# Each attention score matmul in two 32x64 tiles instead of one 32x128 tile

## The chip, the cores and the metric

One core of a Trainium2 chip runs the kernel. The metric is the time of one execution on the device, in microseconds (us). A profile was taken of one execution with the hardware profiler. TensorE (PE) does the matmuls and loads their weights (PEld), VectorE (DVE), ScalarE (ACT) and GpSimd (POOL) work on tiles in the on-chip memories, and SyncE (SP) issues DMAs.

## The reference

Two transformer layers, each windowed attention and then a feed-forward part, with the same weights in both layers. Sequence 2048, model width 576, 32 heads of 18, a window of 256 keys, feed-forward width 4608. The inputs are bf16.

```python
def _A_ref(x, wqkv, wo):
    B, S, D = x.shape
    H = 32; Dh = D // H; W = 256
    qkv = (lambda x, *d: x.transpose(*d))((x @ wqkv).reshape(B, S, 3, H, Dh), 2, 0, 3, 1, 4)
    q, k, v = qkv[0], qkv[1], qkv[2]
    scores = jnp.einsum("bhqd,bhkd->bhqk", q, k) * (Dh ** -0.5)
    idx = jnp.arange(S)
    mask = (idx[:, None] - idx[None, :] >= 0) & (idx[:, None] - idx[None, :] < W)
    scores = jnp.where(mask[None, None], scores, -1e9)
    p = _softmax(scores, axis=-1)
    o = jnp.einsum("bhqk,bhkd->bhqd", p, v)
    return (lambda x, *d: x.transpose(*d))(o, 0, 2, 1, 3).reshape(B, S, D) @ wo
...
    x = x + _A_ref(_layernorm(x, axis=-1), A_wqkv, A_wo)
    x = x + _B_ref(_layernorm(x, axis=-1), B_w1, B_b1, B_w2, B_b2)
```

`_B_ref` is a second layernorm, a matmul to 4608, gelu, and a matmul back to 576. The last two lines come twice.

## The kernel before

**Tiling.** The sequence is cut into chunks of 512 queries (four tiles of 128), four per layer, eight in all. For a chunk the kernel does layernorm and transposes, queries, keys and values (`qkv`, matmuls at lines 779, 782, 798 and 838), attention (`E`, made of `scores` and `pv`), the output projection and residual (`tail`), the first feed-forward matmul with gelu in three parts (`G_part`, matmuls at line 1074), and the second in three parts (`mm2`, through the helper `quad`, lines 779 and 782). Parts of neighbouring chunks are interleaved, so that attention of one chunk stands among feed-forward work of the one before.

**Scores.** Heads are laid out 32 partitions apart: group `g` of eight holds four heads, head `j` in partitions 32j to 32j+31 of `qT` and `kT` (18 of them are values, the others are zero). A task of `scores` takes one group and one unit of blocks. A unit is one or two parts, each one key tile of 128 keys against one, two or three neighbouring query tiles: 384 and 128 columns, 256 and 256, or, at a layer's start, 384 alone or 256 and 128. For each part four matmuls (line 907) run side by side in four row tiles of TensorE: head `j` in rows 32j, all 128 keys as its columns, written to a PSUM bank of its own (`bs[j // 2]` is a pair of banks). Such four are called a set below. The weights are the keys, the moving operand is the queries. ScalarE then takes the exponential of each pair of banks (line 916) into `pT`, GpSimd masks diagonal blocks and blocks at the window's edge (line 937), and `pv` (line 954) multiplies with the values in four column tiles: head `j` writes partitions 32j to 32j+19, 20 columns of weights, of which one is ones and gives the sum of the softmax.

**Other tile shapes.** Line 779 uses the whole array (128 x 128) and line 782 the same work in four column tiles of 128 x 32; `quad` takes one or the other by what stands next to it. Lines 838 and 1074 use two row tiles of 64 x 128, which share the contraction of 576 in halves. The page writes a shape as rows*columns of the weights ahead of the moving operand's.

**Order.** Work is added as tasks to a planner (`Plan`). Each has an estimated cost, data dependences, a priority with a written-out nudge by stage, and a mode that stands for its tile shape ("r" for scores, "c" for column tiles, "h" for two row tiles, "f" for the whole array); a change of mode adds 0.095 us to the estimate. The planner sorts the tasks into one fixed order per engine and gives each PSUM banks; the estimates decide nothing at run time. A task's matmuls are issued together, and the last of them signals the task's semaphore. Its waits stand before the first.

Of the kernel before, what the change touches and what calls it, by code (L numbers as in the profile page):

```python
# [40 lines left out]
class Sched:  # L41
# [23 lines left out]
    def add(self, eng, fn, reads=(), writes=(), dma=None, ring=4, own=False):  # L65
        waits = {}

        def want(ev):
            c, v, _e = ev
            if waits.get(c, 0) < v:  # L70
                waits[c] = v

        for r in reads:
            lw = self.last_write.get(r)
            if lw is not None and not (eng == "pe" and lw[2] == "pe"):
                want(lw)
        for w in writes:
            for rd in self.readers.get(w, ()):
                if own or rd[2] != eng or rd[3]:
                    want(rd[:3])  # L80
            lw = self.last_write.get(w)
            if lw is not None and (own or not (eng == "pe" and lw[2] == "pe")):
                want(lw)
        if dma is None:
            assert eng != "sp"
            c = self.cnt[eng]
            amount = 1
        else:
            rg = self.ring(eng, dma, ring)
            c = rg.sems[rg.i % rg.k]  # L90
            rg.i += 1
            amount = 16
            if c.val > 0:
                want((c, c.val, None))
        wl = []
        wd = self.waited[eng]
        for cc, v in waits.items():
            if wd.get(cc, 0) >= v:
                continue
            wd[cc] = v  # L100
            wl.append((cc, v))
        c.val += amount
        by = None if dma is not None else eng
        ev = (c, c.val, by)
        self.steps[eng].append(Step(eng, fn, wl, c, amount))
        for w in writes:
            self.last_write[w] = ev
            self.readers[w] = []
        for r in reads:
            self.readers.setdefault(r, []).append((c, c.val, by, dma is not None))  # L110
        return ev
# [323 lines left out]
def build_kernel(nc, A_x, A_wqkv, A_wo, B_x, B_w1, B_b1, B_w2, B_b2, out):  # L435
# [158 lines left out]
    def two(b):  # L594
        return ps[:, b.no * 512:(b.no + 2) * 512].rearrange("p (j c) -> p j c", j=2)
# [18 lines left out]
    def q_of(k):  # L614
        return (qx, "qx") if k == 1 else (qT, "q")

    def k_of(A):

        if Q1 <= A < Q1 + 2:
            return kx[:, A - Q1, :, :], f"kx{A - Q1}"  # L620
        sl = A if A < Q1 else (A - 2) % KS
        return kT[:, :, sl, :], f"k{sl}"
# [273 lines left out]
    def scores(k, g, parts, prio):  # L896
        l, t0, nt = CH[k]
        T0 = l * NT + t0
        qs, qname = q_of(k)
        sl = slots.popleft()  # L900
        bs = [Bank(SC, True), Bank(SC, True)]

        def fn(e):
            ins = None
            for (so, qo, nq, col) in parts:
                for j in range(4):
                    ins = e.matmul(two(bs[j // 2])[:, j % 2, col:col + nq * 128], k_of(T0 + so)[0][32 * j:32 * j + 32, g, :],  # L907
                                   qs[32 * j:32 * j + 32, g, qo * 128:(qo + nq) * 128], start=True, stop=True, tile_position=(32 * j, 0))
            return ins
        rd = [f"{qname}{qo + i}" for (so, qo, nq, col) in parts for i in range(nq)] + [k_of(T0 + p[0])[1] for p in parts]  # L910
        ncol = sum(p[2] for p in parts) * 128
        add("pe", fn, reads=rd, writes=bs, cost=0.01 + ncol * 0.00042, prio=prio, lat=0.15, alloc=bs, fifo="pa", mode="r", after=[f"p{sl}h{h}" for h in range(2)] + [f"p{sl}m{m}" for m in range(3)])
        lo = min(p[3] for p in parts)
        hi = max(p[3] + p[2] * 128 for p in parts)
        for h2 in range(2):
            add("act", lambda e, h2=h2: e.activation(pT[:, sl, 2 * h2:2 * h2 + 2, lo:hi], two(bs[h2])[:, :, lo:hi],  # L916
                                                     ACT.Exp, scale=SCALE),
                reads=[bs[h2]], writes=[f"p{sl}h{h2}"], cost=0.07 + 2 * (hi - lo) * 0.00083, lat=0.17,
                fifo="act", prio=prio)
        blk = {}  # L920
        for (so, qo, nq, col) in parts:
            for q in range(nq):
                if qo + q == so:
                    blk[col + q * 128] = "d"
                elif qo + q == so + 2:
                    blk[col + q * 128] = "o"
        runs = []
        for c in sorted(blk):
            if runs and runs[-1][0] == blk[c] and runs[-1][1] + runs[-1][2] * 128 == c:
                runs[-1][2] += 1  # L930
            else:
                runs.append([blk[c], c, 1])
        for mi, (kind, col, nb) in enumerate(runs):
            sgn = 1 if kind == "d" else -1
            pat = [[0, 4]] + ([[0, nb]] if nb > 1 else []) + [[sgn, 128]]
            ap = pT[:, sl, :, col:col + nb * 128]
            add("pool", lambda e, ap=ap, pat=pat, sgn=sgn, kind=kind: e.affine_select(  # L937
                ap, ap, pattern=pat, compare_op=(ALU.is_ge if kind == "d" else ALU.is_gt), fill=0.0, base=0, channel_multiplier=-sgn),
                reads=[f"p{sl}h0", f"p{sl}h1"], writes=[f"p{sl}m{mi}"], cost=0.12 + 0.475 * nb, prio=prio)
        return sl  # L940
# [373 lines left out]
```

## Time and profile before

| | |
|---|---|
| median of three runs | 863.52 us (863.37 to 866.63) |
| the profiled execution's own time | 865.5 us |
| its span, from the first to the last instruction | 863.7 us |
| granted TensorE clock | 1.000 |
| TensorE matmuls, busy | 849.0 us, 12056 |
| ScalarE, busy | 593.3 us |
| VectorE, busy | 391.1 us |
| GpSimd, busy | 378.7 us |
| line 907 (scores), matmuls | 1216, and 192 more whose operands lie in other tiles |

A row of a group names line, engine, operation, the tiles written and read, the shape, the number of instructions, then busy time and the mean ns of one, then idle time of the engine just before them with what ended it. Busy time counts overlapping instructions once. Matmuls are pipelined and the end of each is modelled, so rows of the timeline overlap by some 0.1 to 0.2 us; starts are what to compare. A row of a single line in a short window gives the minimum, median and maximum duration in ns. The row of waits gives total us, number and longest.

### The profile page before, as it was taken

The page shows a single profiled execution, that of the slowest core. Times are in us where ns is not written, and L with a number is a line of the kernel's source. Part 1 is how long each engine was busy: PE and PEld are TensorE (multiplying, and loading weights), DVE is VectorE, ACT ScalarE, POOL GpSimd, SP SyncE. Part 2 cuts the span into 40 slices and gives each one's busy share as a digit, 9 for nine tenths or more (in the row PEclk, how much of TensorE's full clock was granted, in tenths as well). Part 3 has the DMA queues.
Part 4 walks back from the last instruction along what each step waited for, and adds up shares of the span by engine and source line. Part 5 has one row for each costly group of instructions (what it writes and reads, how often), then busy time and mean ns, then how long its engine had stood idle before and what let it go on. Part 6 is the DMA issues. An engine that isn't in the chain of part 4 may idle for free.

```text
span 863.7 us, 27936 instructions
## 1 busy us (share of the span) xinstructions
PE 849.0 (98%) x12056; PEld 523.2 (61%) x12056; DVE 391.1 (45%) x934; ACT 593.3 (69%) x741; POOL 378.7 (44%) x560
## 2 busy tenths in 40 slices
PE   9899999999999999999999999999999999999998
PEld 7555556656556565565655665756556655656556
DVE  5879324645227542393424832655234434244012
ACT  5986787868767588573875776737787589872730
POOL 3876544565135653264421863425454276222100
PEclk9999999999999999999999999999999999999999
DMA  9598445351585715947359443684536953455320
GB/s 238 139 201 145 122 126 148 107 162 45 164 175 112 165 43 165 189 108 170 92 149 215 107 122 124 112 180 99 172 97 127 297 141 108 134 162 147 123 83 28
DMA packets 181866, 119.83 MB, mean 139 GB/s; under 512 B 107440, under 2 KB 181744, under 8 KB 181744
## 3 DMA queue, kind: packets, MB, share of 16 engines
q1 hardware_dynamic: 181744, 118.05, 54.8%
q8 instruction: 95, 1.56, 0.8%
q14 instruction: 27, 0.22, 0.1%
HBM read 90.10 MB, written 2.36 MB: 107 GB/s over the span
## 4 chain that ended last, share of the span: by engine, by line
PE 92%; DMA 2%; POOL 2%; ACT 2%; issue 1%; DVE 1%; POOLq 0%; ACTq 0%
PE ps L1074 32%; PE ps L779 28%; PE ps L782 11%; PE ps L838 9%; PE ps L907 6%; PE ps L954 5%; DMA xnTa<-xn 2%; POOL pT L937 2%; ACT pT L916 1%; PE ps L798 1%; PE ps L681 1%; DMA qT<-qn 1%; DVE oq L965 0%; ACT hT L1084 0%; PE ps L672 0%
## 5 line engine op out<-in xcount | busy, mean ns | idle before, releaser
L937 POOL TENSOR_SCALAR_AFFINE_SELECT pT<-pT 128x512 bf16<-128x512 bf16 (+1 forms) x368 | 284.0, 793 | 255.8 <-ACT pT L916 250.7
L916 ACT ACTIVATE pT<-ps 128x1024 bf16<-128x1024 f32 (+1 forms) x384 | 345.1, 973 | 59.1 <-PE ps L907 58.5
L1074 PE MATMUL ps<-xnTm,w_sb 64*128 64x512 bf16 x2592 | 290.5, 376 | 1.1 <-DVE x_res L1017 0.3
L1084 ACT ACTIVATE hT<-ps,b1col 128x512 bf16<-128x512 f32 x276 | 167.6, 688 | 174.9 <-PE ps L1074 174.4
L1074 PEld LDWEIGHTS ps<-xnTm,w_sb 64*128 64x128 bf16 x2592 | 128.3, 94 | 143.4 <-issue 6.9
L779 PE MATMUL ps<-w_sb,hT 128*128 128x288 bf16 x1410 | 188.8, 287 | 0.0
L1017 DVE TENSOR_TENSOR x_res<-ps,x_res 128x288 f32<-128x288 f32 x224 | 100.1, 450 | 189.0 <-PE ps L779 160.2
L779 PEld LDWEIGHTS ps<-w_sb,hT 128*128 128x128 bf16 x1410 | 130.8, 98 | 48.6 <-issue 15.1
L782 PE MATMUL ps<-w_sb,hT 128*32 128x288 bf16 x2808 | 96.2, 286 | 1.5 <-issue 1.4
L838 PE MATMUL ps<-wqkv,xnTa 64*128 64x288 bf16 x1296 | 91.3, 283 | 2.0 <-DMA xnTa<-xn 1.8
L965 DVE STREAM_TRANSPOSE oq<-ps 128x512 f32<-128x512 f32 x64 | 45.7, 715 | 99.5 <-PE ps L954 98.9
L859 DVE CAST qn<-ps 128x288 bf16<-128x288 f32 x120 | 49.0, 451 | 81.5 <-PE ps L838 66.5
L782 PEld LDWEIGHTS ps<-w_sb,hT 128*32 128x32 bf16 x2808 | 72.4, 97 | 16.6 <-issue 5.8
L838 PEld LDWEIGHTS ps<-wqkv,xnTa 64*128 64x128 bf16 x1296 | 61.8, 94 | 31.0 <-DMA xnTa<-xn 2.7
L907 PE MATMUL ps<-qT,kT 32*128 32x384 bf16 (+2 forms) x1216 | 64.1, 276 | 1.5 <-ACT pT L916 0.9
L694 DVE BATCH_NORM_STATS2 st_all<-x_res 128x6 f32<-128x288 f32 (+1 forms) x128 | 53.5, 442 | 5.0 <-DMA x_res<-in_A_x_dram 4.1
L1090 POOL TENSOR_TENSOR x_res<-x_res,b2bc 128x576 f32<-128x576 f32 x32 | 40.2, 1277 | 32.8 <-ACT hT L1084 32.8
L846 DVE CAST vA<-ps 128x288 bf16<-128x288 f32 x64 | 26.7, 451 | 61.7 <-PE ps L838 59.9
L707 POOL TENSOR_SCALAR vtmp<-mv_all 128x1 f32<-128x1 f32 (+1 forms) x43 | 8.9, 208 | 102.2 <-DVE mv_all L698 99.4
L954 PE MATMUL ps<-pT,vA 128*20 128x384 bf16 (+2 forms) x1408 | 50.4, 275 | 1.0 <-POOL pT L937 0.7
L907 PEld LDWEIGHTS ps<-qT,kT 32*128 32x128 bf16 x1216 | 19.4, 92 | 41.8 <-issue 26.6
L954 PEld LDWEIGHTS ps<-pT,vA 128*20 128x20 bf16 x1408 | 28.0, 91 | 18.5 <-issue 6.4
(58 smaller groups left out, 481.6 us busy)
## 6 DMA issues: line engine op xcount, KB each, us to landing
w_sb<-in_B_w_dram SPq DMA_DIRECT2D x46, 864.0 KB, 6.2
w_sb<-in_B_w_dram SPq DMA_DIRECT2D x48, 768.0 KB, 4.8
w_sb<-in_B_w_dram SPq DMA_DIRECT2D x96, 48.0 KB, 4.5
wqkv<-in_A_wqkv_dram SPq DMA_DIRECT2D x3, 576.0 KB, 4.5
x_res<-in_A_x_dram SPq DMA_DIRECT2D x3, 576.0 KB, 4.8
wqkv<-in_B_w_dram SPq DMA_DIRECT2D x2, 864.0 KB, 5.5
out_dram<-x_res SPq DMA_DIRECT2D x12, 144.0 KB, 2.0
wo_sb<-in_A_wo_dram SPq DMA_DIRECT2D x4, 144.0 KB, 3.2
```

The lines of the kernel that those rows point to most:

```text
L694: add("dve", lambda e, i=i, s=s: e.bn_stats(st_all[:, t, i, :], s[:, t, i * HB:(i + 1) * HB]), reads=res, writes=[f"st{t}_{i}"], cost=0.37 ...
L779: return e.matmul(bank(b)[:, 0:HB], lhs, rhs, start=start, stop=stop, skip_group_check=True)
L782: ins = e.matmul(bank(b)[32 * j:32 * j + 32, 0:HB], lhs[:, 32 * j:32 * j + 32], rhs, start=start, stop=stop, tile_position=(0, 32 * j), sk ...
L838: ins = e.matmul(bank(bs[o])[:, 0:HB], xnTa[r:r + 64, c, i * 128:(i + 1) * 128], wqkv[r:r + 64, c, col:col + HB], start=(c == 4), stop=(ph ...
L859: add("dve", lambda e, b=bs[o], dst=dst: e.tensor_copy(dst, heads_of(bank(b))), reads=[bs[o]], writes=[f"qn{sl}h{o}"], cost=0.375, lat=0.1 ...
L907: ins = e.matmul(two(bs[j // 2])[:, j % 2, col:col + nq * 128], k_of(T0 + so)[0][32 * j:32 * j + 32, g, :], qs[32 * j:32 * j + 32, g, qo * ...
L916: add("act", lambda e, h2=h2: e.activation(pT[:, sl, 2 * h2:2 * h2 + 2, lo:hi], two(bs[h2])[:, :, lo:hi], ACT.Exp, scale=SCALE), reads=[bs ...
L937: add("pool", lambda e, ap=ap, pat=pat, sgn=sgn, kind=kind: e.affine_select(ap, ap, pattern=pat, compare_op=(ALU.is_ge if kind == "d" else ...
L954: ins = e.matmul(bank(bo)[32 * j:32 * j + VW, qo * 128:(qo + nq) * 128], vA[:, (T0 + so) % VS, 8 * j + g, :], pT[:, sl, j, col:col + nq * ...
L1017: add("dve", lambda e: e.tensor_tensor(x_res[:, t, sl], bank(b)[:, 0:HB], x_old[:, t, sl], ALU.add), reads=[b] + ([f"xin{t}"] if first els ...
L1074: ins = e.matmul(bank(bks[i])[:, 0:n], w1_sb[r:r + 64, sls[i], col:col + 128], xnTm[r:r + 64, k % 2, c, 0:n], start=(c == 4), stop=(ph == ...
L1084: add("act", lambda e, ff=ff, hd=hd, bk=bk: e.activation(hd[:, 0:n], bank(bk)[:, 0:n], ACT.Gelu_apprx_tanh, bias=b1col[:, ff:ff + 1]), rea ...
```

## The change

In `scores`, each matmul becomes two. The first computes the lower 64 keys and writes partitions 0 to 63, the second the upper 64 keys and partitions 64 to 127, of the same bank and the same columns. Their tile position is row 32j and column 0 or 64. The moving operand (the queries) is the same for both. The task's cost, waits, banks and place in the order are as before, and so is all that reads the scores. A set has eight matmuls and eight weight loads instead of four and four.

```diff
                 for j in range(4):
-                    ins = e.matmul(two(bs[j // 2])[:, j % 2, col:col + nq * 128], k_of(T0 + so)[0][32 * j:32 * j + 32, g, :],
-                                   qs[32 * j:32 * j + 32, g, qo * 128:(qo + nq) * 128], start=True, stop=True, tile_position=(32 * j, 0))
+                    for u in range(2):
+                        ins = e.matmul(two(bs[j // 2])[64 * u:64 * u + 64, j % 2, col:col + nq * 128],
+                                       k_of(T0 + so)[0][32 * j:32 * j + 32, g, 64 * u:64 * u + 64],
+                                       qs[32 * j:32 * j + 32, g, qo * 128:(qo + nq) * 128], start=True, stop=True, tile_position=(32 * j, 64 * u),
+                                       skip_group_check=True)
```

## The prediction

> **What bounds the kernel now.** I read the page's engine rows first, then its groups, then the timeline of TensorE alone, then single lines inside short windows, then what TensorE waits for.
>
> ```profile
> PE 849.0 (98%) x12056; PEld 523.2 (61%) x12056; DVE 391.1 (45%) x934; ACT 593.3 (69%) x741; POOL 378.7 (44%) x560
> PEclk9999999999999999999999999999999999999999
> q8 instruction: 95, 1.56, 0.8%
> L907 PE MATMUL ps<-qT,kT 32*128 32x384 bf16 (+2 forms) x1216 | 64.1, 276 | 1.5 <-ACT pT L916 0.9
> ```
>
> TensorE is busy 98% of the span at full granted clock, and no other engine passes 69%. A busy share can hide pipelining, so I checked that the stream is really dense. The timeline shows it:
>
> ```profile
> 310.81 0.29 PE L838 MATMUL ps<-wqkv,xnTa 64*128 64x288 bf16 x2
> 311.03 0.40 PE L907 MATMUL ps<-qT,kT 32*128 32x256 bf16 x8
> 311.35 0.83 PE L954 MATMUL ps<-pT,vA 128*20 128x384 bf16 x24
> 312.01 1.65 PE L782 MATMUL ps<-w_sb,hT 128*32 128x288 bf16 x48
> 313.59 0.40 PE L907 MATMUL ps<-qT,kT 32*128 32x384 bf16 x8
> 313.92 1.65 PE L779 MATMUL ps<-w_sb,hT 128*128 128x288 bf16 x12
> 315.50 0.40 PE L907 MATMUL ps<-qT,kT 32*128 32x384 bf16 x8
> ```
>
> Starts are the numbers to use, since modelled ends overlap the next burst. From 312.01 to 313.59, 48 matmuls in four column tiles (12 sets) take 1.58 us; from 313.92 to 315.50, 12 full-width ones take 1.58 us too. Instruction by instruction the trace gives 122.5 ns from set to set in both: 288 columns at 2.4 per ns plus 2.5 ns. So four column tiles stream truly side by side. A score task (8 matmuls in 2 sets of four row tiles, 512 columns) holds TensorE from 311.03 to 311.35, 0.32 us: 213 ns of streaming, and the rest is the change of tile shape. Adding columns and the changes of shape accounts for almost the whole span, so any nanosecond added to a score task goes to the end.
>
> Count of tasks: 1216 + 128 + 64 = 1408 score matmuls (the rows by shape) make 352 sets in 192 tasks; each task has another tile shape before it and after it.
>
> **The change, part by part.** Nothing is moved: task order, waits, buffers and the instruction order of every engine stay, since the planner's costs are untouched. 1408 matmuls with their loads become 2816; columns per matmul stay. The reads of the scores by ScalarE are the same size.
>
> *Streaming.* Eight tiles run where four ran. No row shows row and column tiles together. The nearest rows are the four row tiles of line 907 and the four column tiles of line 782, both at full rate, the latter with four separate moving streams of 128 partitions. Two streams in each of four row groups is less. I take 0; the other end (pairs taking turns) is a rival below.
>
> *The exposed weight load.* The first set after a change of shape waits for its weights; later loads hide under streaming. The duration of a set shows it:
>
> ```profile
> L907 PE MATMUL ps<-qT,kT x8: 267/273/278, 311.0 to 311.2; 32*128 32x256 bf16 x8
> L782 PE MATMUL ps<-w_sb,hT x24: 286/286/297, 175.9 to 176.5; 128*32 128x288 bf16 x24
> ```
>
> Minimum, median and maximum: the first set of scores takes 278 ns and the second 267; the first set of 32-column tiles 297 against 286. So 10 to 11 ns are exposed for 128 columns in row tiles, and as much for 32 columns in column tiles. The 20-column tiles of line 954, entered after scores, show 331 to 332 against 326 ns, 5.5 ns. Among column tiles the load thus grows by 5 ns for 12 columns, 0.42 ns each; 32 further columns give 10.5 + 13.3 = 24 ns, or **+13.3 ns** per task. That is +2.55 us for 192 tasks. The ends: half of today's 10.5 ns (-5 ns, -1.0 us) if a load went by its columns regardless of tiling, and two such loads in a row group one after the other (+37 ns, +7.2 us). I take the line through the two column-tile rows, being the nearest.
>
> The Trainium skill ("TensorEngine Tiling (Array Packing)", Restrictions and Gotchas) says that column tiling rules out the fast weight load; by that rule 128 columns now load fast and 64 would not. The equal exposure of 128 and 32 columns agrees with it. By this rule the term stays near +2.55 us; without it, a load that goes by its columns alone would make the term -1.0 us.
>
> *The tail of a set.* Matmuls of one set start 3 to 4 ns apart (311.027, .030, .034, .037 in the window above), so the eighth starts about 24 ns after the first where the fourth started 10. The next shape waits for the last to drain. Start to start, less the columns streamed, a change of shape takes 98 ns after sets of one, 103 after the four row tiles and 108 to 109 after four column tiles: between half and all of the skew shows. For 14 ns more skew that is +7 to +14; I take 12 ns, +2.3 us. Ends: 0 (the skew hides in the drain) and +2.7 us.
>
> *Instruction supply.* TensorE's instructions arrive by DMA, 1.56 MB in 95 packets, about 256 instructions each. In two places TensorE ran dry:
>
> ```profile
> PE ps L782 <- issue: 2.6, 2, 1.4
> ```
>
> The first is at 265.81 us, 1.35 us long, in a dense stretch of column tiles; the packet that ended it started at 263.13, and the one before at 247.23. The second, 1.24 us at 567.56, looks the same (packets at 559.05 and 565.05). 2816 more instructions make 11 more packets and let dense stretches use them up faster. By packets alone, 2.6 us x 11/95 is +0.3 us. I counted, for each packet of this trace, the instructions used between its start and the place where those two stalls ran dry, with the score instructions doubled: one to two more packets come too late, at 1.3 us each. I take +1.6 us; the ends are +0.3 and +3.9 (three more stalls).
>
> **Sum.** 2.55 + 2.3 + 1.6 = +6.4 us on the profiled execution's 865.5 us (span 863.7, 1.8 us around it): 871.9. That execution stands 2.0 us above the median of the runs, 863.52, so the time to compare is 869.9; I say **870 us**, +0.75%. The other engines hide nothing here: scores are followed by other TensorE work that does not need them, so the delay is TensorE's own. What waits for scores (ScalarE, 58.5 us idle for line 907 in all) sees them some 25 ns later, against waits of hundreds of ns. With the low end of all three terms the time is 862.8; with the high ends, 877.3.
>
> **Rivals.**
>
> 1. *The load is not longer and the skew hides.* 128 and 32 columns expose the same 10.5 ns today, so the exposure could be a floor that 64 columns share, and the row-tiled sets already hide half their skew. Taken to its end, where a load goes by its columns alone, 64 instead of 128 gain 5 ns at each entry of a score task: 863.5 - 1.0 + 0.3 = 862.8; with the floor, 863.8 to 865. It decides from the point where the first set's exposure stays at or under 10.5 ns. Against it: 20 columns expose half of what 32 do, so there is no floor there. The Trainium skill ("TensorE: Matmul & The Clock Gate", LDWEIGHTS) gives a load by its columns alone; by that, 32 columns should have exposed a quarter of what 128 do, and the trace shows them equal. This is the case that ends not slower.
>
> 2. *The two halves of a pair take turns.* Both read the same 32 partitions of queries and write the same bank. If their streams exclude each other, each set takes its columns twice: (128 x 384 + 112 x 256 + 112 x 128) / 2.4 = 38.4 us more, about 908 us. Against it: four column tiles at line 782 read the same 128 partitions and write one bank, at full rate.
>
> 3. *Supply takes over.* If four or more further packets come late, +5 us and more on top of load and skew: 873.5 to 877. For it: both stalls of today lie in dense stretches; against it: only 2 packets of 95 were late enough.
>
> 4. *The tiles are not what the source says*, or some order shifts: then nothing changes, 863.5. The instruction order speaks against it.
>
> **How the numbers follow.** Forecast (866 to 873.5 us): 0.62. Rival 1: 0.22. Rival 2: 0.09. Rival 3: 0.06. Rival 4: 0.01. The range takes in the forecast, rival 3 and the upper part of rival 1: 863.5 to 877, leaving out rival 2 and the gaining end of rival 1. What a measurement of this kernel can tell from no change is about 0.5%, 4.3 us, so 859.2 to 867.8 counts as the same: nearly all of rival 1, rival 4 and the lower edge of the forecast, 0.29. Faster 0.02. Slower 0.69.
>
> **What would show it.** In the changed profile the score group has 2816 matmuls and loads; busy time of that line rises by some 5 us, not 38. In short windows, the first set of scores stands about 24 ns above the second in duration (11 now); a score task of 512 columns lasts 0.35 us from its start to the next burst (0.32 to 0.33 now). Four-tile column sets keep 122.5 ns. TensorE's wait by issue grows from 2.6 us by one or two entries. A score task of 0.54 us would prove rival 2; one of 0.32 us, rival 1; many issue waits, rival 3. The forecast is wrong as well if queues of the other engines turn out to follow the scores closely, which would show as longer waits of ScalarE on line 907's successor than today's 58.5 us.

## The result and the profile after

The changed kernel takes 872.8 us (median of five runs, 870.95 to 874.63); the kernel before, on the same chip and in the same session, 864.18 us (863.37 to 868.12). The ratio is 1.0099, with a 95% interval of 1.008 to 1.0117. A second measurement gave 1.0083 (1.0053 to 1.0113), a third, with 144 instructions more at the head, 1.0078 (1.0053 to 1.0104). It is slower by 0.8 to 1%; forecast was 0.75%.

The changed kernel's profiled execution took 872.8 us, its span 871.0. Lines of its page, engines, instruction packets and the two groups of the scores:

```profile
PE 854.1 (98%) x13464; PEld 533.0 (61%) x13464; DVE 392.3 (45%) x934; ACT 595.7 (68%) x741; POOL 376.8 (43%) x560
q8 instruction: 106, 1.74, 0.8%
L908 PE MATMUL ps<-qT,kT 32*64 32x384 bf16 (+2 forms) x2432 | 69.1, 284 | 3.5 <-DMA qT<-qn 1.5
L908 PEld LDWEIGHTS ps<-qT,kT 32*64 32x64 bf16 x2432 | 25.4, 102 | 44.1 <-issue 29.4
```

Scores have twice the matmuls and their busy time rises from 64.1 to 69.1 us. TensorE alone is busier; the other engines hardly move. The stretch of the timeline that was shown of before starts 3.5 us later now:

```profile
314.50 0.42 PE L908 MATMUL ps<-qT,kT 32*64 32x256 bf16 x16
314.85 0.83 PE L957 MATMUL ps<-pT,vA 128*20 128x384 bf16 x24
315.51 1.64 PE L782 MATMUL ps<-w_sb,hT 128*32 128x288 bf16 x48
317.09 0.42 PE L908 MATMUL ps<-qT,kT 32*64 32x384 bf16 x16
317.44 1.64 PE L779 MATMUL ps<-w_sb,hT 128*128 128x288 bf16 x12
319.02 0.42 PE L908 MATMUL ps<-qT,kT 32*64 32x384 bf16 x16
```

Again starts count: a score task holds TensorE 0.35 us (314.50 to 314.85) where it was 0.32 to 0.33, and 12 sets of line 782 or 12 matmuls of line 779 still take 1.58 us. If the two halves took turns, the task would take 0.54 us. Durations in one short window (minimum, median, maximum):

```profile
L908 PE MATMUL ps<-qT,kT x16: 267/280/292, 320.9 to 321.1; 32*64 32x256 bf16 x16
```

The second set takes 267 ns as before, the first 292 where it took 278: by durations, 25 ns of weight load are exposed instead of 11 (the starts in the table below give 2 ns more, as a set whose load is hidden also starts 2.5 ns beyond its columns after the one ahead). And what TensorE waits for:

```profile
PE ps L1077 <- DMA xnTm<-xn: 2.4, 2, 2.0
PE ps L782 <- issue: 2.3, 2, 1.6
PE ps L908 <- DMA qT<-qn: 1.5, 1, 1.5
PE ps L908 <- ACT pT L919: 1.4, 6, 0.3
...
PE ps L908 <- issue: 0.5, 1, 0.5
```

Waits for instructions did not grow in sum (3.2 us with small ones, 3.3 before). A new wait of 2.0 us stands on top: the first feed-forward matmul waits for a transpose.

Read instruction by instruction from the starts, as medians over the tasks, in ns beyond the columns streamed (columns / 2.4; the last row is for a task of 512 columns with its own 213 ns in it):

| | before | after |
|---|---|---|
| change of shape into the scores, from the full array | 98 | 96 |
| first set to second | 13 | 26.5 |
| first start to last start in a set | 10 | 23 |
| change of shape out of the scores, to the full array | 103 | 117 |
| a whole task between its neighbours' streams | 427 | 452 |

Tasks of 384 columns grow by 25 ns as well (373 to 398), so 192 tasks make 4.8 us. The spans differ by 7.3. ScalarE's idle time for the scores, a sign that the prediction named, went from 58.5 to 61.1 us.

### The profile page after: what moved, and what is told of

Read it like the earlier page. It is cut to its first block, busy times and chain, and to the rows that moved or that the text cites. A ratio compares the mean times of both kernels' runs of the same rounds, so it can differ in the third digit from the quotient of the medians.

```text
span 871.0 us, 30752 instructions
## 1 busy us (share of the span) xinstructions
PE 854.1 (98%) x13464; PEld 533.0 (61%) x13464; DVE 392.3 (45%) x934; ACT 595.7 (68%) x741; POOL 376.8 (43%) x560
## 4 chain that ended last, share of the span: by engine, by line
PE 90%; ACT 3%; DMA 3%; issue 2%; DVE 1%; POOL 0%; DVEq 0%; POOLq 0%
PE ps L1077 32%; PE ps L779 26%; PE ps L782 10%; PE ps L838 9%; PE ps L908 7%; PE ps L957 4%; ACT pT L919 3%; DMA xnTm<-xn 2%; PE ps L798 1%; PE ps L681 1%; DMA x_res<-qn 1%; DMA qT<-qn 1%; DVE xn L719 0%; DVE qn L859 0%; ACT hT L1087 0%
## 5 line engine op out<-in xcount | busy, mean ns | idle before, releaser
L919 ACT ACTIVATE pT<-ps 128x1024 bf16<-128x1024 f32 (+1 forms) x384 | 347.5, 970 | 62.1 <-PE ps L908 61.1
L908 PE MATMUL ps<-qT,kT 32*64 32x384 bf16 (+2 forms) x2432 | 69.1, 284 | 3.5 <-DMA qT<-qn 1.5
L846 DVE CAST vA<-ps 128x288 bf16<-128x288 f32 x64 | 26.7, 451 | 61.1 <-PE ps L838 59.0
L908 PEld LDWEIGHTS ps<-qT,kT 32*64 32x64 bf16 x2432 | 25.4, 102 | 44.1 <-issue 29.4
```

The source lines that it names most:

```text
L908: ins = e.matmul(two(bs[j // 2])[64 * u:64 * u + 64, j % 2, col:col + nq * 128], k_of(T0 + so)[0][32 * j:32 * j + 32, g, 64 * u:64 * u + 6 ...
```

## The experiments

**What makes the exposed load longer: width, or two tiles in a row group?** `lower64` has the narrow load without the second half:

```diff
+        kw = 64 if k >= 2 else 128
...
-                    for u in range(2):
-                        ins = e.matmul(two(bs[j // 2])[64 * u:64 * u + 64, j % 2, col:col + nq * 128],
+                    for c0, cw in ((0, kw),):
+                        ins = e.matmul(two(bs[j // 2])[c0:c0 + cw, j % 2, col:col + nq * 128],
...
-            add("act", lambda e, h2=h2: e.activation(pT[:, sl, 2 * h2:2 * h2 + 2, lo:hi], two(bs[h2])[:, :, lo:hi],
+            add("act", lambda e, h2=h2: e.activation(pT[0:kw, sl, 2 * h2:2 * h2 + 2, lo:hi], two(bs[h2])[0:kw, :, lo:hi],
```

> From the third chunk on (144 of the 192 score tasks), only the lower 64 keys of each block are scored, in four 32x64 tiles per set; ScalarE reads and writes 64 partitions there, so the upper 64 keys of the probabilities are stale. Number of instructions and skew of a set are those of before; only the weight load is 64 columns in a column tile. Theory A (a load outside the full 128 columns takes time by its columns, 0.42 ns each): the second set starts N/2.4 + 26 ns after the first (13 before, 26 to 27 with the change), the change of shape behind stays at 103, so +13 ns x 144 = +1.9 us, about 865.5. Rival B (two loads or two streams in one row group get in each other's way, width has no part): N/2.4 + 13 ns, and 863.5, no change.

First to second set is 26.5 ns in all chunks from the third on and 13 in the first two; the change of shape behind is 103 throughout. Its durations in one window:

```profile
L909 PE MATMUL ps<-qT,kT x8: 267/280/292, 171.3 to 171.5; 32*64 32x256 bf16 x8
```

The same 267 and 292 as with eight tiles. The time was 1.0019 of before (1.0003 to 1.0036), +1.6 us against 1.9 forecast. Theory A holds: four tiles of 64 columns expose as much as eight.

**How the load goes with the columns.** The same edit, with a width for each chunk.

```diff
+        kw = (128, 128, 20, 32, 48, 64, 96, 112)[k]
```

> Chunks 2 to 7 score only the first 20, 32, 48, 64, 96 and 112 keys of each block, one chunk each, with one matmul per head; the other keys of the probabilities are stale. Read from the start of a task's first set to its second, beyond N/2.4. Theory A1 (anything but 128 columns loads slowly, 0.42 ns per column): 8, 13, 20, 26, 40 and 46 ns. Theory A2 (column tiling is what makes it slow; 96 and 112 columns fill the width of a 32x128 tile and load fast): 8, 13, 20, 26, then 13 and 13 or less. Rival B (width has no part): 13 throughout. Only the trace is read.

Measured: 8, 13, 20, 26.5, 40 and 47 ns, which is columns / 2.4 in each case, and 13 for 128 columns. One window of 256-column sets for 20, 32, 64, 96 and 112:

```profile
L909 PE MATMUL ps<-qT,kT x8: 267/270/273, 169.6 to 169.7; 32*20 32x256 bf16 x8
```
```profile
L909 PE MATMUL ps<-qT,kT x8: 267/272/278, 276.1 to 276.2; 32*32 32x256 bf16 x8
```
```profile
L909 PE MATMUL ps<-qT,kT x8: 267/280/292, 474.7 to 474.8; 32*64 32x256 bf16 x8
```
```profile
L909 PE MATMUL ps<-qT,kT x8: 267/286/305, 589.6 to 589.7; 32*96 32x256 bf16 x8
```
```profile
L909 PE MATMUL ps<-qT,kT x8: 267/290/312, 695.2 to 695.3; 32*112 32x256 bf16 x8
```

The minimum, a set whose load is hidden, never moves. The maximum climbs by 0.42 ns per column up to 112, and at 128 it is back at 278, as for 32. So it is A1: column for column, 128 columns expose a quarter of what any other width tried does. Nothing is left over for column tiles as such: 20, 32 and 64 columns lie on one line with 96 and 112, which are wider than any column tile here. The Trainium skill ("TensorE: Matmul & The Clock Gate", Weight-path perf modes) turns the fast load on at 128 weights; the trace agrees, 13 ns at 128 against 47 at 112. The rule on column tiling that the prediction cited gives the right answer for the changed kernel, but would not have given 40 ns for 96 columns.

**The tail, and four tiles in a row group.** `tiles16` cuts each score matmul in four of 32 keys.

```diff
-                    for u in range(2):
+                    for u in range(4):
```

(and 32 in place of 64 in the slices and positions.)

> Each score matmul as four, in 32x32 tiles, sixteen to a set, in all 192 tasks. The load is 32 columns, so first to second set should be back at N/2.4 + 13 ns, as before the change. Sixteen starts 3.4 ns apart put the last 51 ns behind the first: if the tail counts in full, the change of shape behind goes from 103 (four) and 117 (eight) to about 144; if only part of it counts or the drain hides it, to 117 to 130. Score tasks then cost +39 ns x 192 = +7.5 us against before (+3 to +5 if it hides). Rival (pairs or fours in one row group take turns at this width): 160 ns more for a set of 384. Supply: 8448 more instructions, 33 more packets. If density decides, waits by issue rise from 3 us to 6 or more and the time to 877 or more; if they stay at 2 to 5 us, supply was not what the change paid with.

First to second set is 13, the last start 50 ns behind the first, the change of shape out 144: load and tail come out apart, each as the theory has it, and no halves or quarters take turns. The task takes 465 ns against 427, +7.3 us in all. Yet the kernel took 889.27 us, 1.0252 of before (1.0221 to 1.0283), some 22 us more. Its waits:

```profile
PE ps L782 <- issue: 6.6, 6, 2.1
PE ps L908 <- DMA kT<-qn: 3.1, 1, 3.1
...
PE ps L957 <- issue: 1.8, 1, 1.8
PE ps L1077 <- DVE attT L978: 1.8, 1, 1.8
```

Waits for instructions are 9.9 us in all (with 1.1 at the scores and some small ones) against 3.3, other waits before 150 us 12.4 against 7.5. With 33 packets more, instruction supply is a cost of its own; with the 11 of the change it is not to be told from chance: 3.2, 2.5, 3.6 and 1.1 us in the four traces of the whole change, 3.3 and 2.7 in the two of before, and 4.7 in `lower64`, which has no packet more. Of the 25 us by which the span of `tiles16` grew, tasks and these waits make about 19. The trace also shows two stretches of 3.41 us, from 41.3 and from 72.0 us on, with the granted clock at 0.5, behind TensorE waits of 1.8 and 3.1 us; full-width matmuls of 288 columns start 240 ns apart there and 122.5 outside, so each stretch costs at most 1.7 us. The remaining 3 us or so were not followed.

**Order of the two halves.** `u_outer` exchanges the loops.

> The change with its two loops exchanged: the four lower halves first, then the four upper ones. If two neighbours in one row group got in each other's way, the first set or the tail would move. By load and tail alone nothing does: 26 to 27 ns and 117 ns. Only the trace is read.

26.5 ns, 117 ns and 452 ns a task, as in the change. The order within a set has no part.

**Where the rest is lost: early chunks, late chunks, the whole again.**

```diff
-                    for u in range(2):
+                    for c0, cw in (((0, 64), (64, 64)) if k >= 2 else ((0, 128),)):
```

(`late`; `early` has `k < 2`, and `whole` is the change unaltered.)

> The change in chunks 2 to 7 alone (144 of 192 tasks), the first two chunks as before. If the score tasks alone carry the cost, 25 ns x 144 = +3.6 us and no more, about 867.8. If the waits for transfers in the first 130 us carry the rest of the change's +8.6 us, they are as before here. If instruction supply carries the rest, one or two more waits by issue after 130 us, +1.3 to +2.6 us on top, about 870.

> The change in the first two chunks alone (48 of 192 tasks). Score tasks alone: 25 ns x 48 = +1.2 us, about 865.3. If the rest of the change's cost lies in the waits for transfers of the first 130 us, where those tasks stand, +3 to +4 us, about 867 to 868. Instruction supply gives nothing here that can be told.

> The change once more, with more runs. Score tasks by the trace: +25 ns x 192 = +4.8 us. The two parts measured alone gave +2.8 and +2.9 us, 5.7 together, against +8.5 in the first measurement. If the rest beyond 4.8 is a cost of the change (supply, or a shift of transfers), it stays at +7 to +9; if it is chance in the waits for transfers and instructions, it comes out at +5 to +6.

`late` 1.0032 (1.0016 to 1.0048), +2.8 us; `early` 1.0033 (1.0013 to 1.0052), +2.9 us; `whole` 1.0083, +7.2 us. A quarter of the tasks costs as much as the other three quarters. For `late`, 3.6 us lies inside the interval. For `early`, 1.2 us lies at its lower edge, so times alone leave it nearly open. `whole` at +7.2 us lies where a cost of the change was put, but its interval of +4.6 to +9.8 us holds the other case too. The traces tell a part. All four with the change in the first two chunks up to here (the first profile, `whole`, `u_outer` and `early`) wait about 2 us for the transposes into `xnTm`, near 89 us; `late`, `lower64`, `widths` and before do not. But `late`, whose first two chunks are as before and whose early waits were expected to be so too, has a wait of 3.8 us at 57 us, and its waits other than for instructions before 150 us are 10.0 us, against 7.5 before and 9.3 with the whole change. So the wait for `xnTm` goes with the change in the early chunks, and the sum of the early waits does not. In the timeline of the changed kernel and, below, of before:

```profile
85.77 1.38 PE L838 MATMUL ps<-wqkv,xnTa 64*128 64x288 bf16 x16
89.13 1.24 PE L1077 MATMUL ps<-xnTm,w_sb 64*128 64x512 bf16 x9 [1.98 <-DMA xnTm<-xn]
```
```profile
84.61 1.51 PE L838 MATMUL ps<-wqkv,xnTa 64*128 64x288 bf16 x18
86.41 1.90 PE L1074 MATMUL ps<-xnTm,w_sb 64*128 64x512 bf16 x16 [0.28 <-DVE attq L971]
```

**A stretch at half the clock.** The trace of `late` shows what a long wait can bring with it. Behind its 3.8 us at 57 us the granted clock is 0.5 for 3.41 us (second line, a window of 3 us: the third figure from its end is the clock):

```profile
57.00 1.38 PE L779 MATMUL ps<-wqkv,xnTa 128*128 128x288 bf16 x5 [3.76 <-DVE qn L859]
57.20:60.20 3.00, 3.00 (x16) 1.48 (x15) 1.81 (x6) 1.33 (x2) 1.28 (x2) 0.50 0.55 106
```

Such a stretch stands in the traces of `early` (274 us, behind a wait of 2.5 us), `shift_after` (58 us) and `shift_before2` (592 us, both behind a wait of 2.4 us) too, and in none of before, the first profile and `u_outer`. It does not always follow: waits of 2.4 us in `before_b` and 2.8 us in `lower64` had none behind them. Half the clock for 3.41 us takes the mean clock of an execution to 0.998. In the measurement of `late` and `early` the kernel before took 865.1 us on average at 1.000 (24 executions) and 867.7 at 0.998 (5); `late` took 867.3 (7) and 870.8 (5), `early` 867.6 (7) and 870.0 (5). At 1.000 alone the two parts thus cost +2.2 and +2.5 us, a little less than above. The traces of both are of executions at 0.998, near the upper end of their times.

**Why the transpose is late.** In those four traces a packet of instructions (16 KB, which holds one DMA engine about 1 us) starts 1.2 to 2.3 us behind the issue of the last transpose. The packets of the DMA queue then show nearly all of that transpose's data done, and the last few completion writes 1 to 2 us later, behind the instruction packet. More instructions earlier on had brought the packet to that place. To move packets without touching a score, I cut the zero-filled filler matmuls of the first 10 us, whose result is unused:

```diff
-        for _ in range(n):
-            ins = e.matmul(bank(bk)[:, 0:256], warm[:, :], warm[:, :].unsqueeze(1).to_broadcast([P, 2, P]), start=True, stop=True)
+        for _ in range(3 * n):
+            ins = e.matmul(bank(bk)[:, 0:86], warm[:, :], warm[:, 0:86], start=True, stop=True)
```

(`shift_before2` has `3 * n + n // 2` of 73 columns.)

> The kernel before the change, with each filler matmul of the first 10 us (zeros, result unused) cut into three of 86 columns: 72 matmuls or 144 instructions more at the head, no score task touched. Instruction packets then start some 5 us earlier; the one at 90.26 us would start near 85.5, some 2 us behind the issue of the last transpose into xnTm (83.37), as it does wherever the first two chunks are changed (84.7 to 87.8). Theory P (a packet of instructions among a transpose's work makes it land late): TensorE waits about 2 us for xnTm at 87 to 89 us, 0.3 before, and that transpose lands over 4 us after its issue instead of 2.6. Rival Q (the wait comes from the score tasks' own delay in the first chunks): none appears. The time stays within 0.3%.

> The change, with the same 144 instructions more at the head. Its packet of 86.26 us would start near 82, ahead of the last transpose into xnTm. Theory P: the wait of 2.0 to 2.2 us for xnTm that every run with the first two chunks changed has shown is gone or under 0.6 us; waits may turn up at another transfer. Rival Q: it stays at about 2 us. The score tasks keep their +25 ns, so the time stays over that of before, +5 to +8 us.

> The kernel before the change with 178 to 180 instructions more at the head (filler matmuls of 73 columns). With 144 the packet started at 86.61 us, 2.3 us behind the issue of the last transpose into xnTm and just as that landed; 34 more put it about 1.2 us earlier, among the transpose's own packets. Theory P: that transpose lands over 4 us after its issue, its last completion packets behind the instruction packet, and TensorE waits 1 to 2 us for xnTm at 88 to 90 us, with no score task changed. Rival Q: 2.6 us, and no such wait. Only the trace is read.

> The kernel before the change once more, for a second trace: how far the waits for transfers and for instructions move from one execution to the next. If they are fixed by the order, 7.6 us of other waits before 150 us, none of 2 us for xnTm, and 3.3 us by issue again; if chance has a hand, 6 to 10 and 2 to 5.

Times in us from each span's start:

| kernel | last transpose into xnTm issued | landed | instruction packet near it | TensorE's wait for it |
|---|---|---|---|---|
| before | 83.37 | 85.95 | none (81.07, 90.26) | none |
| before_b | 83.72 | 86.30 | none (81.21, 90.48) | none |
| after | 84.32 | 88.67 | 86.26 | 2.0 |
| whole | 83.52 | 87.82 | 84.69 | 2.1 |
| u_outer | 84.33 | 88.50 | 85.93 | 2.1 |
| early | 85.48 | 89.95 | 87.79 | 2.2 |
| shift_after | 87.11 | 89.69 | 85.53 | none |
| shift_before | 84.29 | 86.88 | 86.61 | none |
| shift_before2 | 84.79 | 88.17 | 85.70 | none |

`shift_after` did as theory P has it, though in part by another way than planned: its packet came only 0.7 us earlier than in the change (85.53 against 86.26), and the last transpose was issued 2.8 us later (87.11 against 84.32), behind a wait of 2.4 us at 57 us. The packet fell on the first of the last three transposes instead, which landed 4.15 us after its issue (83.67 to 87.82); the last, undisturbed, took 2.58, and the wait near 89 us is gone (one of 1.2 us stands at 796 us):

```profile
88.45 1.52 PE L838 MATMUL ps<-wqkv,xnTa 64*128 64x288 bf16 x18
90.15 2.12 PE L1077 MATMUL ps<-xnTm,w_sb 64*128 64x512 bf16 x18 [0.18 <-DVE attq L974]
```

The two that were to make the wait appear missed. In `shift_before` the packet started when all 32 completion writes of the transpose were done, so it proves nothing. In `shift_before2` it fell on the transpose before the last (issued 83.47, landed 87.75, 4.28 us), and the last took 3.38; but TensorE had other work to 88.3 us, so nothing waited. That the packet makes the transpose late is borne out by all 13 traces. They hold 411 transposes of `xn` into `xnTm` whose landing can be read. The 62 with a packet that starts 1.0 to 2.2 us behind the issue take 3.6 to 4.8 us to land, with a median of 4.2; the 191 with no packet from 1.5 us ahead of the issue to the landing have a median of 2.58, and nine in ten take less than 2.8. The two traces of before have 12 of the late kind, with 4.2 us as well. So lateness goes with the packet, whether scores are changed or not, and the wait near 89 us was there in the four traces with such a packet on the last transpose and gone in the one where transpose and packet had moved apart. That moving a packet alone makes that wait in the kernel before was tried twice and not reached.

The 2 us were not simply added to the time. Other waits in the first 100 us come and go: `shift_after` waits 2.4 us for queries being copied at 57 us instead (as `late` did, 3.8 us), has a stretch at half the clock behind it, and 1.0078 of before is hardly less than the change. `shift_before` was 1.0029 (1.0013 to 1.0045), +2.5 us with no score touched, which I had put within 0.3%. Its trace is of the fastest of its ten executions (865.06, span 863.3), so where the 2.5 us lie is not shown. Waits other than for instructions before 150 us are 7.5 and 7.4 us in the two traces of before, and 9.3, 8.9, 9.4 and 8.7 in the four of the whole change: +1.6 us on average. Traces whose early score tasks are those of before run from 6.3 (`widths`) to 10.0 (`late`), so it is not shown that these 1.6 us are a lasting cost of the change.

## Why the prediction was right, point by point

- *TensorE sets the end, so what a score task gains goes to the end.* Right. The task grew by 25 ns, 4.8 us in all, and nothing hid it.
- *Streaming, 0.* Right: the second set stays at 267 ns, and sixteen tiles run side by side as well as eight. Rival 2 is out.
- *Exposed load, +13.3 ns, +2.55 us.* Right to the digit: 13 to 26.5. The line through 20 and 32 columns was the law. Column tiling, the reason that the prediction named for it, is not what decides: 96 and 112 columns lie on the same line and are too wide for a column tile here. The entry gives 2 ns back (96 against 98), which I had not seen; `lower64` and `widths` show it at every width but 128, so it belongs to the load, whose net is 11.5 ns. Rival 1, a floor or a gain, is out: 13, 20 and 26.5 ns for 32, 48 and 64 columns.
- *Tail, 12 ns, +2.3 us.* Nearly: 14 ns more (117 against 103), so all of the skew shows and not part of it, as at sixteen tiles (144). The 12 were a choice between 7 and 14. That load and tail together come to 25 ns, as forecast, is luck to the extent of 2 ns: one term was 2 too high and the other 2 too low.
- *Instruction supply, +1.6 us.* This is the step that failed. TensorE ran dry no longer than before, within what changes from one execution to the next (1.1 to 3.6 us against 2.7 and 3.3). In its place the traces of the change have 1.6 us more of other waits in the first 150 us. That the size agrees is luck. The part that was followed comes from the same packets by another way: one falls among the packets of a transpose that TensorE waits for. Whether the rest comes with the change at all stays open. Rival 3 by its own mechanism came only with three times as many instructions added.
- *The sum.* 4.8 + 1.6 makes 6.4 us, as forecast, by a partly different route; four spans with the change lie at 869.4 to 871.6 us against 863.7 and 863.6, +6.8 on average. Measured were +8.6, +7.2 and, with the shift, +6.7 us, with intervals of about 1.6 to 2.6 us to either side. That the first measurement is 2 us above the traces is not explained: two of its five executions, 873.6 and 874.63 us, were at a mean clock of 0.998, but the other three still have a mean of 871.8 us.

## What to carry to other kernels

Cutting a matmul into more tiles of the array cost no streaming time here, with up to sixteen, but it is paid twice at each change of tile shape: the first load is exposed by its columns / 2.4 ns unless it has 128, and each further matmul of the last set holds the next shape back by some 3.4 ns. Read both from the first and second set's duration and from start-to-start times, and look at neighbouring shapes in the same trace: three widths gave the price here before anything ran. In a kernel at 98% of one engine with transfers just in time, added instructions also move the packets that bring them, and a packet that falls among the packets of a transfer can delay it by 1.5 us or more; what that costs in the end has to be measured more than once.

## What was not expected of the hardware

- Weight loads of 20, 32, 48, 64, 96 and 112 columns expose 8, 13, 20, 26.5, 40 and 47 ns, and 128 columns 13.
- A transpose of 2.6 us lands after 3.6 to 4.8 us, with a median of 4.2, when a packet of about 256 instructions (16 KB, about 1 us on one DMA engine) starts 1.0 to 2.2 us behind its issue.
- 144 filler instructions more in the first 10 us moved the time by +0.13 to +0.45%. By the 2.5 ns that a matmul takes beyond its columns, their own length is an estimated 0.2 us; the rest is not explained.
- Behind TensorE waits of 1.8 to 3.8 us the granted clock was 0.5 for 3.41 us in five of the 13 traces, and matmuls of 288 columns started 240 ns apart instead of 122.5.
